# Attention parts ordered one per half unit, units of slice 0 first for two batches, four kv buffers, exponential in place, q loaded in token halves

## The chip, the cores and the metric

The kernel runs on one core of one Trainium2 chip. The metric is the time of one execution on the device in microseconds (us). Before the change it is 1198.53 us, the median of three runs (1197.06 to 1201.19).

## The reference

The program computes three stages in fp32, one after the other.

```python
# attention: B=4 batches, H=8 heads, S=576 tokens, D=64, M=32 memory slots
a  = softmax(phi, over tokens)                      # exp(phi - max), divided by its sum
km = einsum('bhsm,bhsd->bhmd', a, k)                # pooled keys
vm = einsum('bhsm,bhsd->bhmd', a, v)                # pooled values
attn = softmax(q @ km^T / 8)                        # 32 scores for each token and head
x = (attn @ vm) as [2304 tokens, 512]
# first feed-forward: w_in [512, 2048], w_out [2048, 512], given in float64
h = x @ w_in;  x = (h * cos(h)) @ w_out
# second feed-forward: 4 experts, w1 [512, 1024], w2 [1024, 512], weighted by p
out = sum over e of p[:, e] * (relu(x @ w1[e]) @ w2[e])
```

## The kernel before, in words

**Attention.** The eight heads are two groups g of four heads (`HG`). A batch b has four tiles of work in that order: `pool_exp(b, g)` (L173) takes phi, forms the exponential on ScalarE (ACT) and transposes it on TensorE (PE) into `es`; `pool_kv(b, g)` (L193) multiplies `es` by the loaded k and v into `kvp`, scales, transposes and leaves the pooled keys in `kT` and the pooled values in `vT`; `scores(b, g, split_th)` (L225) multiplies `kT` by q, and then runs a softmax as a chain that goes from engine to engine: VectorE (DVE) transposes and takes the maximum, GpSimd (POOL) subtracts, ACT takes the exponential, DVE sums and inverts, POOL multiplies, DVE transposes back, ACT and POOL split the result into a high and a low part (`attnT`). In what follows, a part is `pool_kv(b, g)` with `scores(b, g)`. There are eight parts.

**First feed-forward.** The 2048 hidden columns are cut into eight slices s of 256. A unit is a pair (s, b), and the list `order` (L350) gives the 32 units their sequence; before, slices 0 and 1 of a batch stand one behind the other, batch by batch, and from slice 2 on each slice runs over all four batches. `project(ns)` (L281) folds the pooled values into w_in for one or two units (`vw`). `step1(n, ahead)` (L353) runs a unit in two halves th of 288 tokens: `hidden1` (L303) is 12 matmuls into `hp` and then the cosine on ACT and DVE (its first ACT instruction stands in L319, so L319 counts the halves); `output1` (L327) is 24 matmuls into `op`, added to `acc` by DVE. `output1` runs two halves behind `hidden1` (`pend`). During the attention `op` is one PSUM bank for 128 of the 512 columns, so there are four accumulations a half (128x288); once the attention's PSUM pools are closed, `op` is two banks and there are two accumulations of 128x576. `load_in` and `load_out` (L268, L273) load a slice of weights in two chunks each, and `narrow` (L107) turns float64 into fp32 with one ACT and three DVE instructions a chunk.

**What sets the order.** The program order of the loop at L389 is a priority: the program is planned with a timeline before it runs (L652), and on each engine the earliest instruction in program order that is ready in that timeline is put next. The instructions of several parts and units are thus mixed, and each engine's queue is fixed when the program starts. In the loop, for b = 1 to 3, come both `pool_exp(b, .)`, the unit 2b-2 whole, part (b, 0), part (b, 1), and the unit 2b-1 whole; units 2b-2 and 2b-1 belong to batch b-1. After the loop come the units from 6 on.

**Buffers.** `kv` and `kvt` have three buffers, and a batch uses four (two for each g). `phi` has three and `ex`, the exponential, two. `q` has two, one for a whole batch. All those loads are issued on SyncE's queue (SP), in one sequence.

**Second feed-forward** (L432 to L605) follows, and the change does not touch it.

Of the kernel before, what the change touches and what calls it, by code (L numbers as in the profile page):

```python
# [9 lines left out]
F32 = mybir.dt.float32  # L10
# [14 lines left out]
def tile_kernel(  # L25
# [11 lines left out]
    out: bass.AP,  # L37
):
    nc = tc.nc
    B, HG, S = qt_in.shape[0], qt_in.shape[2], qt_in.shape[3]  # L40
    D = 64
    M = 32
    NT, DM = out.shape
# [100 lines left out]
    cs = cs_ctx.enter_context(tc.tile_pool(name="cs", bufs=2))  # L144
    at_ctx = ExitStack()
    attnT = [mb.tile([128, 2, 2, S], F32R, tag=f"attnT{b}", name="attnT") for b in range(B)]
    vT = mb.tile([128, HG, B, M], F32, tag="vT", name="vT")
    at = at_ctx.enter_context(tc.tile_pool(name="att", bufs=1, side="right"))

    exps = []  # L150
# [7 lines left out]
    def load_kv(b, g):  # L158
        kvs_in[b, g] = []
        for h in range(2):  # L160
            t = at.tile([128, NC, 2, 2 * D], F32, tag="kv", name="kv", bufs=3)
            nc.sync.dma_start(out=t, in_=kv_in[b, g, h])
            t2 = at.tile([TAIL, 2, 2 * D], F32, tag="kvt", name="kvt", bufs=3)
            nc.sync.dma_start(out=t2, in_=kvt_in[b, g, h])
            kvs_in[b, g].append((t, t2))

    def load_q(b):
        qs[b] = at.tile([128, HG, S], F32, tag="q", name="q", bufs=2)
        nc.sync.dma_start(out=qs[b], in_=qt_in[b])

    kTs, ees = {}, {}

    def pool_exp(b, g):  # L173
        ph = phs[b, g]
        nmx = at.tile([128, 1], F32, tag="nmx", name="nmx", bufs=2)
        nc.vector.tensor_reduce(out=nmx, in_=ph, axis=AX.X, op=ALU.max)
        nc.vector.tensor_scalar_mul(nmx, nmx, -1.0)
        ex = at.tile([128, S], F32, tag="ex", name="ex", bufs=2)
        rs = at.tile([128, 1], F32, tag="rs", name="rs", bufs=2)
        nc.scalar.activation(out=ex, in_=ph, func=ACTF.Exp, bias=nmx, accum_out=rs)  # L180
        nc.vector.tensor_scalar_add(rs, rs, 1e-9)
        nc.vector.reciprocal(out=rs, in_=rs)
        es = at.tile([128, NC + 1, 128], F32, tag="es", name="es", bufs=2)
        pe = ps_c.tile([128, NC, 128], F32, tag="c", name="pe")
        for c in range(NC):
            nc.tensor.transpose(pe[:, c, :], ex[:, 128 * c:128 * c + 128], ident)
        nc.scalar.copy(out=es[:, :NC], in_=pe)
        pt = ps_c.tile([128, 128], F32, tag="c", name="pt")
        nc.tensor.transpose(pt[:TAIL], ex[:, 128 * NC:], ident)
        nc.vector.tensor_copy(out=es[:TAIL, NC], in_=pt[:TAIL])  # L190
        ees[b, g] = es, rs

    def pool_kv(b, g):  # L193
        es, rs = ees[b, g]
        kv = kvs_in[b, g]
        p0 = 64 * g
        kvp = ps_c.tile([128, 2 * D], F32, tag="c", name="kvp")
        for c in range(NC + 1):
            n = 128 if c < NC else TAIL
            for i in range(HG):  # L200
                nc.tensor.matmul(  # L201
                    out=kvp[32 * i:32 * i + 32],
                    lhsT=es[:n, c, 32 * i:32 * i + 32],
                    rhs=kv[i // 2][0][:, c, i % 2] if c < NC else kv[i // 2][1][:, i % 2],
                    start=c == 0,
                    stop=c == NC,
                )
        kvs = at.tile([128, 2, 2, D], F32, tag="kvs", name="kvs", bufs=2)
        nc.scalar.activation(
            out=kvs,  # L210
            in_=kvp.rearrange("p (t d) -> p t d", t=2)[:, :, None, :].to_broadcast([128, 2, 2, D]),
            func=ACTF.Copy,
            scale=rs,
        )
        pkt = ps_c.tile([128, 2, 128], F32, tag="c", name="pkt")
        for x in range(2):
            nc.tensor.transpose(pkt[:, x], kvs[:, x].rearrange("p u d -> p (u d)"), ident)
        if g == 0:
            kTs[b] = at.tile([128, HG * M], F32, tag="kT", name="kT", bufs=2)
        nc.vector.tensor_scalar_mul(kTs[b][p0:p0 + 64], pkt[p0:p0 + 64, 0], qk_scale)  # L220
        nc.vector.tensor_copy(
            out=vT[p0:p0 + 64, :, b, :], in_=pkt[p0:p0 + 64, 1].rearrange("p (i m) -> p i m", i=HG)
        )

    def scores(b, g, split_th):  # L225
        aT, p0 = attnT[b], 64 * g
        kT, qT = kTs[b], qs[b]
        st_all = at.tile([128, S // 32, 32], F32, tag="st", name="st", bufs=2)
        smx_all = at.tile([128, S // 32], F32, tag="smx", name="smx", bufs=2)
        ssm_all = at.tile([128, S // 32], F32, tag="ssm", name="ssm", bufs=2)  # L230
# [1 line left out]
        for ths in ((0,), (1,)) if split_th else ((0, 1),):  # L232
            blk = slice(9 * ths[0], 9 * ths[-1] + 9)
            st, smx, ssm = st_all[:, blk], smx_all[:, blk], ssm_all[:, blk]
            nb = st.shape[1]
            for th in ths:
                sc = ps_o.tile([128, 512], F32, tag="o", name="sc")
                for i in range(HG):
                    nc.tensor.matmul(
                        out=sc[32 * i:32 * i + 32, :TH],  # L240
                        lhsT=kT[p0:p0 + 64, 32 * i:32 * i + 32],
                        rhs=qT[p0:p0 + 64, i, th * TH:th * TH + TH],
                        start=True,
                        stop=True,
                    )
                nc.vector.transpose(
                    out=st_all[:, 9 * th:9 * th + 9, :].rearrange("p a b -> p (a b)"), in_=sc[:, :TH]
                )
            nc.vector.tensor_reduce(out=smx, in_=st, axis=AX.X, op=ALU.max)
            nc.gpsimd.tensor_tensor(  # L250
                out=st, in0=st, in1=smx[:, :, None].to_broadcast([128, nb, 32]), op=ALU.subtract
            )
            exps.append(nc.scalar.activation(out=st, in_=st, func=ACTF.Exp))
            nc.vector.tensor_reduce(out=ssm, in_=st, axis=AX.X, op=ALU.add)
            nc.vector.tensor_scalar_add(ssm, ssm, 1e-9)
            nc.vector.reciprocal(out=ssm, in_=ssm)
            nc.gpsimd.tensor_tensor(
                out=st, in0=st, in1=ssm[:, :, None].to_broadcast([128, nb, 32]), op=ALU.mult
            )
            cols = slice(TH * ths[0], TH * ths[-1] + TH)  # L260
            nc.vector.transpose(out=stT_all[:, cols], in_=st.rearrange("p a b -> p (a b)"))
            split(aT[:, 0, g, cols], aT[:, 1, g, cols], stT_all[:, cols], nc.gpsimd)
# [18 lines left out]
    def project(ns):  # L281
        ps = ps_h.tile([128, 2, 512], F32, tag="h", name="vw_ps")
        for j, n in enumerate(ns):
            s, b = order[n]
            for i in range(HG):
                for g in range(2):
                    nc.tensor.matmul(  # L287
                        out=ps[32 * i:32 * i + 32, g, j * FS:j * FS + FS],
                        lhsT=vT[64 * g:64 * g + 64, i, b, :],
                        rhs=wi[s][64 * g:64 * g + 64, i, :],  # L290
                        start=True,
                        stop=True,
# [54 lines left out]
    vws = {}  # L347
    ops_ = [ps_o]
    pend = []
    order = [(s, b) for b in range(B) for s in range(2)]  # L350
    order += [(s, b) for s in range(2, NS1) for b in range(B)]

    def step1(n, ahead):  # L353
        s, b = order[n]
        for th in range(2):
            if n > 8 and b in (1, 2) and s + 1 < NS1:
                (load_in, load_out)[b - 1](s + 1, marks[-1], th)
            pend.append((s, b, th, hidden1(b, th, vws[n]), wo[s]))
            if len(pend) > 2:
                output1(*pend.pop(0))  # L360
            if th == 0 and ahead:
                project(ahead)

    warm = ps_o.tile([128, 512], F32, tag="o", name="warm")
# [1 line left out]
    def warm_up(n):  # L366
        for _ in range(n):
            nc.tensor.matmul(out=warm[:, :128], lhsT=ones, rhs=ones, start=True, stop=True)  # L368

    load_phi(0)  # L370
    load_kv(0, 0)
# [3 lines left out]
    for g in range(2):  # L375
        pool_exp(0, g)
    load_in(0)
    load_out(0)
    load_in(1)
    load_phi(1)  # L380
    for g in range(2):
        pool_kv(0, g)
        scores(0, g, True)
    load_kv(1, 0)
    load_kv(1, 1)
    load_out(1)
    load_q(1)
    project((0, 1))
    for b in range(1, B):  # L389
        if b + 1 < B:  # L390
            load_phi(b + 1)
        pool_exp(b, 0)
        pool_exp(b, 1)
        step1(2 * b - 2, None)
        pool_kv(b, 0)
        if b + 1 < B:
            load_kv(b + 1, 0)
        scores(b, 0, False)
        pool_kv(b, 1)
        if b + 1 < B:  # L400
            load_kv(b + 1, 1)
            load_q(b + 1)
        scores(b, 1, False)
        step1(2 * b - 1, (2 * b, 2 * b + 1))
    nu = 2 * B - 2
    c_ctx.close()
    ps_p2 = p_ctx.enter_context(tc.tile_pool(name="ps_p2", bufs=2, space=PSUM, reuse_waits="tile"))
    ops_[:] = [ps_p2, ps_p2]
# [1 line left out]
    at_ctx.close()  # L410
    wc = ctx.enter_context(tc.tile_pool(name="wc", bufs=2, side="right", reuse_waits="tile"))
    for n in range(nu, len(order)):
        if n == nu:
            load_in(2)
        if n == nu + 1:
            load_out(2)
        step1(n, (n + 1, n + 2) if n % 2 and n + 2 < len(order) else None)
    for p in pend:
# [192 lines left out]
def _layout(q, k, v, phi, moe_w_in, moe_w_out, moe2_domain_probs, moe2_w1, moe2_w2):  # L611
# [6 lines left out]
    kv = np.concatenate([k, v], axis=3).reshape(B, G, 2, I // 2, S, 2 * D).transpose(0, 1, 2, 4, 3, 5)  # L618
    f = moe_w_in.shape[1]
    return {  # L620
        "qt": q.reshape(B, G, I, S, D).transpose(0, 1, 4, 2, 3).reshape(B, G * D, I, S),
        "kv": kv[:, :, :, :n].reshape(B, G, 2, n // 128, 128, I // 2, 2 * D).transpose(0, 1, 2, 4, 3, 5, 6),
        "kvt": kv[:, :, :, n:],
        "phi": phi.reshape(B, G, I, S, M).transpose(0, 1, 2, 4, 3).reshape(B, G, I * M, S),
# [32 lines left out]
```

## Time and profile before

| | us |
|---|---|
| median of three runs | 1198.53 (1197.06 to 1201.19) |
| the profiled execution's own time | 1199.46 |
| its span, first to last instruction | 1197.7 |
| PE busy | 1154.0 (96%) |
| DVE busy | 822.7 (69%) |
| POOL busy | 519.1 (43%) |
| ACT busy | 471.5 (39%) |

The span is the time on the chip between the first and the last instruction; the profiled execution's own time is 1.76 us more. An engine's busy share is an average over stages with different limits, so it has to be looked at stage by stage. All times of the trace count from the span's start.

### The profile page before, as it was taken

To read this page: it belongs to the slowest core of one execution; us is meant where nothing else is said; L and a number is where in the kernel's file an instruction comes from. 1 tells how busy PE (TensorE), PEld (TensorE's weight loads), DVE (VectorE), ACT (ScalarE), POOL (GpSimd) and SP (SyncE) were. 2 spreads that over 40 slices of the span, in tenths; PEclk is the share of its full clock that TensorE was granted. 3 is DMA by queue.
4 is the path that set the end of the run, shared out by engine and by line. 5 is a ranking of instruction groups with operands and counts; after the bars stand their busy time and mean duration, and the time that the engine had idled before them with its cause. 6 is when DMAs were issued, how large, how long until landed. Compare 5 with 4: busy or idle time off the path is not lost.

```text
span 1197.7 us, 19388 instructions
## 1 busy us (share of the span) xinstructions
PE 1154.0 (96%) x7786; PEld 1034.2 (86%) x7786; DVE 822.7 (69%) x1375; ACT 471.5 (39%) x786; POOL 519.1 (43%) x597
## 2 busy tenths in 40 slices
PE   6889789999999989999999999999999999999998
PEld 4477689999999888888989898988898889989897
DVE  5976858788878886666666666697666666665665
ACT  3673646666657543222322222253223222322220
POOL 2543433233336715434544454447345534544420
PEclk7599899999999989999999999999999999999999
DMA  9820102211212201111111111113111111111102
GB/s 332 288 92 21 36 1 72 67 39 38 71 38 70 71 1 53 37 36 54 53 36 36 53 54 36 36 56 129 36 39 53 52 36 53 53 37 36 54 1 79
DMA packets 38267, 72.85 MB, mean 61 GB/s; under 512 B 2561, under 2 KB 20001, under 8 KB 37665
## 3 DMA queue, kind: packets, MB, share of 16 engines
q1 hardware_dynamic: 33632, 58.99, 15.0%
q10 hardware_dynamic: 4480, 12.58, 3.2%
q8 instruction: 61, 1.00, 0.4%
q0 software_dynamic: 64, 0.04, 0.1%
q14 instruction: 30, 0.24, 0.1%
HBM read 66.88 MB, written 4.72 MB: 60 GB/s over the span
## 4 chain that ended last, share of the span: by engine, by line
PE 85%; DVE 4%; DMA 4%; POOL 3%; issue 2%; ACT 2%; POOLq 0%; ACTq 0%; DVEq 0%
PE op L132 46%; PE hp L132 36%; DMA kv<-in_kv_dram 1%; PE vw_ps L287 1%; DMA raw<-in_w_out_dram 1%; DMA raw<-in_w_in_dram 1%; PE kvp L201 1%; POOL wa L491 1%; POOL gt L89 1%; PE warm L368 1%; DMA raw<-in_w_dram 1%; DVE y L321 0%; DVE y L323 0%; DVE acc L343 0%; DVE raw L118 0%
## 5 line engine op out<-in xcount | busy, mean ns | idle before, releaser
L132 PE MATMUL op<-wb,ht 128*128 128x512 f32 x1728 | 439.9, 396 | 0.0
L132 PEld LDWEIGHTS hp<-x,wa 128*128 128x128 f32 x2688 | 380.6, 189 | 24.0 <-DVE x L448 3.5
L132 PE MATMUL hp<-x,wa 128*128 128x320 f32 (+1 forms) x2688 | 393.3, 295 | 3.1 <-DVE x L448 3.1
L132 PEld LDWEIGHTS op<-wb,ht 128*128 128x128 f32 x1728 | 313.2, 188 | 58.6
L580 DVE SCALAR_TENSOR_TENSOR acc<-op,p_all,acc 128x512 f32<-128x512 f32 x270 | 201.7, 748 | 136.9 <-PE op L132 136.7
L132 PE MATMUL op<-gt,wo 128*128 128x288 f32 x1536 | 227.2, 299 | 9.0 <-DVE acc L343 6.9
L132 PEld LDWEIGHTS op<-gt,wo 128*128 128x128 f32 x1536 | 211.1, 189 | 20.4 <-DVE acc L343 8.6
L96 POOL TENSOR_TENSOR wb<-raw,wb 128x256 fp32r<-128x256 f32 x124 | 90.0, 758 | 224.4 <-ACT wb L94 224.4
L551 ACT ACTIVATE ht<-c 128x256 fp32r<-128x256 f32 (+3 forms) x128 | 71.8, 562 | 283.4 <-DVE c L521 283.4
L89 POOL TENSOR_TENSOR gt<-y,gt 128x576 fp32r<-128x576 f32 x64 | 97.6, 1525 | 190.7 <-ACT gt L88 149.5
L552 DVE SCALAR_TENSOR_TENSOR ht<-c,ht 128x256 fp32r<-128x256 f32 (+3 forms) x128 | 94.5, 738 | 63.0 <-ACT ht L551 63.0
L491 POOL TENSOR_TENSOR wa<-raw,wa 128x256 fp32r<-128x256 f32 x96 | 69.2, 749 | 149.8 <-ACT wa L481 149.8
L132 PE MATMUL hp<-attnT,vw 128*128 128x288 f32 x768 | 119.8, 305 | 9.6 <-DVE y L323 9.6
L132 PEld LDWEIGHTS hp<-attnT,vw 128*128 128x128 f32 x768 | 110.5, 196 | 13.0 <-DVE y L323 8.4
L521 DVE TENSOR_TENSOR c<-hp,u 128x256 f32<-128x256 f32 (+1 forms) x192 | 87.3, 457 | 42.3 <-PE hp L132 37.8
L491 POOL TENSOR_TENSOR wa<-tt,wa 128x256 fp32r<-128x256 f32 x128 | 111.4, 900 | 1.2 <-ACT wa L485 1.2
L345 DVE TENSOR_TENSOR acc<-op,acc 128x576 f32<-128x576 f32 (+1 forms) x120 | 84.9, 711 | 29.4 <-PE op L132 28.2
L528 ACT COPY p<-hp 128x256 f32<-128x256 f32 x64 | 25.5, 399 | 112.9 <-PE hp L132 112.9
L321 DVE SCALAR_TENSOR_TENSOR y<-kk,y 128x576 f32<-128x576 f32 x64 | 55.0, 859 | 15.1 <-ACT kk L320 14.7
L319 ACT ACTIVATE y<-hp 128x576 f32<-128x576 f32 x64 | 41.4, 647 | 47.1 <-PE hp L132 40.1
L481 ACT ACTIVATE wa<-raw 128x512 fp32r<-128x512 f32 x32 | 20.2, 632 | 87.5 <-PE hp L132 85.3
L323 DVE TENSOR_TENSOR y<-hp,y 128x576 f32<-128x576 f32 x64 | 48.0, 750 | 9.1 <-ACT y L322 8.4
(89 smaller groups left out, 914.6 us busy)
## 6 DMA issues: line engine op xcount, KB each, us to landing
raw<-in_w_dram SPq DMA_DIRECT2D x60, 512.0 KB, 3.5
kv<-in_kv_dram SPq DMA_DIRECT2D x16, 512.0 KB, 5.3
raw<-in_w_in_dram ACTq DMA_DIRECT2D x10, 512.0 KB, 3.3
raw<-in_w_out_dram ACTq DMA_DIRECT2D x10, 512.0 KB, 3.3
q<-in_qt_dram SPq DMA_DIRECT2D x4, 1152.0 KB, 8.0
out_dram<-acc SPq DMA_DIRECT2D x18, 256.0 KB, 2.0
raw<-in_w_in_dram SPq DMA_DIRECT2D x6, 512.0 KB, 5.4
raw<-in_w_out_dram SPq DMA_DIRECT2D x6, 512.0 KB, 4.9
```

Source lines behind the costliest of these rows:

```text
L89: (eng or nc.vector).tensor_tensor(out=lo, in0=src, in1=f32(hi), op=ALU.subtract)
L96: (nc.vector if early and c % 512 else nc.gpsimd).tensor_tensor(out=t[:, 1, c:c + 256], in0=src[:, c:c + 256], in1=f32(t[:, 0, c:c + 256]) ...
L132: nc.tensor.matmul(out=ps, lhsT=lt(a), rhs=rt(b), start=first and i == 0, stop=last and i == 2, skip_group_check=more,)
L319: marks.append(nc.scalar.activation(out=y, in_=hv, func=ACTF.Copy, scale=INV_2PI, bias=0.25))
L321: nc.vector.scalar_tensor_tensor(out=y, in0=kk, scalar=ROUND, in1=y, op0=ALU.subtract, op1=ALU.subtract)
L323: nc.vector.tensor_tensor(out=y, in0=hv, in1=y, op=ALU.mult)
L345: nc.vector.tensor_tensor(out=dst, in0=op[:, :, :TH], in1=dst, op=ALU.add)
L491: pool.tensor_tensor(out=wa[:, 1, o], in0=src, in1=f32(wa[:, 0, o]), op=ALU.subtract)
L521: nc.vector.tensor_tensor(out=out, in0=ps[:, :n], in1=sb, op=ALU.add)
L551: nc.scalar.activation(out=ht[:, 0, fc, lo:], in_=c[:, fc, lo:], func=ACTF.Relu)
L552: nc.vector.scalar_tensor_tensor(out=ht[:, 1, fc, lo:], in0=c[:, fc, lo:], scalar=0.0, in1=f32(ht[:, 0, fc, lo:]), op0=ALU.max, op1=ALU.su ...
L580: nc.vector.scalar_tensor_tensor(out=dst, in0=op, scalar=pe, in1=dst, op0=ALU.mult, op1=ALU.add)
```

## The change

The program order of the attention and the first units is written out by hand. A part now alternates with half a unit, and a unit needs a batch that is at least one or two behind the part next to it. The sequence of units becomes (0,0), (0,1), (1,0), (1,1), (0,2), (1,2), (0,3), (1,3). Three whole units (six halves) stand within the attention, where six stood before. `kv` and `kvt` get four buffers, the exponential is written over phi, q comes in two tiles of 288 tokens a batch (four buffers of half the size), and `vT` is one tile for each batch. The loads of slice 2 stay at units 6 and 7.

```diff
-    vT = mb.tile([128, HG, B, M], F32, tag="vT", name="vT")
+    vT = [mb.tile([128, HG, M], F32, tag=f"vT{b}", name="vT") for b in range(B)]
...
-            t = at.tile([128, NC, 2, 2 * D], F32, tag="kv", name="kv", bufs=3)
+            t = at.tile([128, NC, 2, 2 * D], F32, tag="kv", name="kv", bufs=4)
...
     def load_q(b):
-        qs[b] = at.tile([128, HG, S], F32, tag="q", name="q", bufs=2)
-        nc.sync.dma_start(out=qs[b], in_=qt_in[b])
+        for th in range(2):
+            qs[b, th] = at.tile([128, HG, TH], F32, tag="q", name="q", bufs=4)
+            nc.sync.dma_start(out=qs[b, th], in_=qt_in[b, th])
...
-        ex = at.tile([128, S], F32, tag="ex", name="ex", bufs=2)
+        ex = ph
...
-    order = [(s, b) for b in range(B) for s in range(2)]
+    order = [(0, 0), (0, 1), (1, 0), (1, 1), (0, 2), (1, 2), (0, 3), (1, 3)]
...
-    def step1(n, ahead):
+    def step1(n, ahead, ths=(0, 1)):
...
+    def part(b, g):
+        pool_kv(b, g)
+        scores(b, g, b == 0)
...
     load_in(0)
+    load_phi(1)
+    part(0, 0)
+    load_kv(1, 0)
     load_out(0)
+    part(0, 1)
+    load_kv(1, 1)
+    load_q(1)
+    project((0,))
+    for g in range(2):
+        pool_exp(1, g)
     load_in(1)
-    load_phi(1)
+    load_phi(2)
+    part(1, 0)
+    load_kv(2, 0)
+    step1(0, None, (0,))
+    load_out(1)
+    part(1, 1)
+    load_kv(2, 1)
+    load_q(2)
     for g in range(2):
-        pool_kv(0, g)
-        scores(0, g, True)
-    load_kv(1, 0)
-    load_kv(1, 1)
-    load_out(1)
-    load_q(1)
-    project((0, 1))
-    for b in range(1, B):
...
-    nu = 2 * B - 2
+        pool_exp(2, g)
+    step1(0, (1,), (1,))
+    load_phi(3)
+    part(2, 0)
+    load_kv(3, 0)
+    step1(1, (2, 3), (0,))
+    part(2, 1)
+    load_kv(3, 1)
+    load_q(3)
+    for g in range(2):
+        pool_exp(3, g)
+    step1(1, None, (1,))
+    part(3, 0)
+    step1(2, None, (0,))
+    part(3, 1)
+    step1(2, None, (1,))
+    nu = 3
```

## Rows read from the trace of the kernel before

**Rows 1.** The page, the span in 40 equal slices, in tenths.

```profile
PE   6889789999999989999999999999999999999998
...
PEclk7599899999999989999999999999999999999999
```

**Rows 2.** Stretches of the first stage; the header names the columns, (x) are instructions.

```profile
core 0: us, PE busy (x) PEld busy (x) DVE busy (x) ACT busy (x) POOL busy (x), PEclk, DMA share, GB/s
13.00:127.00 114.00, 93.34 (x890) 67.35 (x889) 85.86 (x183) 65.12 (x104) 45.77 (x41) 0.84 0.47 162
127.00:165.00 38.00, 27.58 (x193) 25.52 (x174) 25.29 (x42) 19.01 (x28) 14.71 (x11) 0.87 0.09 28
16.00:55.00 39.00, 27.34 (x224) 16.26 (x224) 33.86 (x84) 19.42 (x37) 15.13 (x18) 0.52 0.92 323
55.00:127.00 72.00, 63.80 (x638) 50.26 (x643) 50.99 (x98) 45.06 (x68) 30.64 (x23) 1.00 0.20 65
170.00:390.00 220.00, 218.04 (x1852) 209.13 (x1851) 179.43 (x254) 140.65 (x210) 85.44 (x67) 1.00 0.17 54
```

**Rows 3.** Timeline of ACT: start, us, what; halves 10 and 16, a table load.

```profile
121.53 1.28 ACT L322 ACT_TABLE_LOAD   x1
...
126.96 0.65 ACT L319 ACTIVATE y<-hp 128x576 f32<-128x576 f32 x1 [1.27 <-PE sc L239]
...
174.97 0.65 ACT L319 ACTIVATE y<-hp 128x576 f32<-128x576 f32 x1
```

**Rows 4.** Chain of waits: start, us, what; the start and 178 to 189 us.

```profile
12.91 11.95 DMA kv<-in_kv_dram
...
178.07 1.60 PE hp L132 x12
179.67 3.20 PE op L132 x24
...
187.65 1.02 PE vw_ps L287 x32
```

**Rows 5.** Timeline, the pooled keys of part (0, 1); in brackets the idle time before.

```profile
24.91 1.92 PE L201 MATMUL kvp<-kv,es 128*32 128x128 f32 x28 [4.44 <-DMA kv<-in_kv_dram]
```

**Rows 6.** DVE by line, 13 to 127 us: count, busy, mean ns.

```profile
L118 DVE SCALAR_TENSOR_TENSOR raw<-raw 128x512 uint32<-128x512 uint32 x10 | 10.0, 1004 | 0.2
L321 DVE SCALAR_TENSOR_TENSOR y<-kk,y 128x576 f32<-128x576 f32 x10 | 9.0, 904 | 3.2 <-ACT kk L320 3.2
L323 DVE TENSOR_TENSOR y<-hp,y 128x576 f32<-128x576 f32 x10 | 7.5, 751 | 3.6 <-ACT y L322 3.6
L345 DVE TENSOR_TENSOR acc<-op,acc 128x288 f32<-128x288 f32 x16 | 7.2, 451 | 4.1 <-PE op L132 3.9
L343 DVE COPY acc<-op 128x288 f32<-128x288 f32 x16 | 7.0, 444 | 4.2 <-PE op L132 4.2
L246 DVE STREAM_TRANSPOSE st<-sc 128x288 f32<-128x288 f32 x14 | 6.4, 471 | 2.6 <-PE sc L239 2.5
L117 DVE TENSOR_SCALAR raw<-raw 128x512 uint32<-128x512 uint32 x10 | 5.2, 524 | 3.7 <-DMA raw<-in_w_out_dram 2.9 <-DMA raw<-in_w_in_dram 0.6
...
L89 DVE TENSOR_TENSOR vw<-vw_ps,vw 128x1024 fp32r<-128x1024 f32 x3 | 3.7, 1222 | 1.5 <-ACT vw L88 1.5
```

**Rows 7.** Timeline of PE and ACT, 124 to 157 us, at the last parts.

```profile
124.35 1.85 PE L132 MATMUL hp<-attnT,vw 128*128 128x288 f32 x12 [0.48 <-DVE y L323]
...
127.44 0.74 PE L239 MATMUL sc<-q,kT 64*32 64x288 f32 x8
...
133.23 3.25 PE L132 MATMUL hp<-attnT,vw 128*128 128x288 f32 x12 [3.50 <-DVE y L323]
...
141.75 1.86 PE L132 MATMUL op<-gt,wo 128*128 128x288 f32 x12 [1.89 <-DVE acc L343]
...
156.50 0.65 ACT L319 ACTIVATE y<-hp 128x576 f32<-128x576 f32 x1 [6.81 <-PE hp L132]
```

**Rows 8.** Queue of SP, 0 to 170 us: total wait, times, longest.

```profile
SPq L162 <- PE kvp L201: 42.4, 9, 19.8
```

More of the change, by code (lines that the diff above doesn't have):

```diff
@@ L39, in tile_kernel @@
     nc = tc.nc
-    B, HG, S = qt_in.shape[0], qt_in.shape[2], qt_in.shape[3]
+    B, HG, S = qt_in.shape[0], qt_in.shape[3], 2 * qt_in.shape[4]
     D = 64
@@ L160, in load_kv @@
         for h in range(2):
-            t = at.tile([128, NC, 2, 2 * D], F32, tag="kv", name="kv", bufs=3)
+            t = at.tile([128, NC, 2, 2 * D], F32, tag="kv", name="kv", bufs=4)
             nc.sync.dma_start(out=t, in_=kv_in[b, g, h])
-            t2 = at.tile([TAIL, 2, 2 * D], F32, tag="kvt", name="kvt", bufs=3)
+            t2 = at.tile([TAIL, 2, 2 * D], F32, tag="kvt", name="kvt", bufs=4)
             nc.sync.dma_start(out=t2, in_=kvt_in[b, g, h])
@@ L221, in pool_kv @@
         nc.vector.tensor_copy(
-            out=vT[p0:p0 + 64, :, b, :], in_=pkt[p0:p0 + 64, 1].rearrange("p (i m) -> p i m", i=HG)
+            out=vT[b][p0:p0 + 64], in_=pkt[p0:p0 + 64, 1].rearrange("p (i m) -> p i m", i=HG)
         )
@@ L226, in scores @@
         aT, p0 = attnT[b], 64 * g
-        kT, qT = kTs[b], qs[b]
+        kT = kTs[b]
         st_all = at.tile([128, S // 32, 32], F32, tag="st", name="st", bufs=2)
@@ L241, in scores @@
                         lhsT=kT[p0:p0 + 64, 32 * i:32 * i + 32],
-                        rhs=qT[p0:p0 + 64, i, th * TH:th * TH + TH],
+                        rhs=qs[b, th][p0:p0 + 64, i, :],
                         start=True,
@@ L288, in project @@
                         out=ps[32 * i:32 * i + 32, g, j * FS:j * FS + FS],
-                        lhsT=vT[64 * g:64 * g + 64, i, b, :],
+                        lhsT=vT[b][64 * g:64 * g + 64, i, :],
                         rhs=wi[s][64 * g:64 * g + 64, i, :],
@@ L349, in tile_kernel @@
     pend = []
-    order = [(s, b) for b in range(B) for s in range(2)]
+    order = [(0, 0), (0, 1), (1, 0), (1, 1), (0, 2), (1, 2), (0, 3), (1, 3)]
     order += [(s, b) for s in range(2, NS1) for b in range(B)]
-    def step1(n, ahead):
+    def step1(n, ahead, ths=(0, 1)):
         s, b = order[n]
-        for th in range(2):
+        for th in ths:
             if n > 8 and b in (1, 2) and s + 1 < NS1:
@@ L360, in step1 @@
                 output1(*pend.pop(0))
-            if th == 0 and ahead:
+            if th == ths[0] and ahead:
                 project(ahead)
@@ L377, in tile_kernel @@
     load_in(0)
+    load_phi(1)
+    part(0, 0)
+    load_kv(1, 0)
     load_out(0)
-    load_in(1)
-    load_phi(1)
-    for g in range(2):
-        pool_kv(0, g)
-        scores(0, g, True)
-    load_kv(1, 0)
-    load_kv(1, 1)
-    load_out(1)
-    load_q(1)
-    project((0, 1))
-    for b in range(1, B):
[L390 to L404, printed above, removed]
-    nu = 2 * B - 2
+    part(0, 1)
[4 more added lines that the diff above has]
+        pool_exp(1, g)
+    load_in(1)
+    load_phi(2)
[6 more added lines that the diff above has]
+    load_q(2)
+    for g in range(2):
+        pool_exp(2, g)
[15 more added lines that the diff above has]
+    nu = 3
     c_ctx.close()
@@ L412, in tile_kernel @@
     for n in range(nu, len(order)):
-        if n == nu:
+        if n == 6:
             load_in(2)
-        if n == nu + 1:
+        if n == 7:
             load_out(2)
@@ L620, in _layout @@
     return {
-        "qt": q.reshape(B, G, I, S, D).transpose(0, 1, 4, 2, 3).reshape(B, G * D, I, S),
+        "qt": q.reshape(B, G, I, 2, S // 2, D).transpose(0, 3, 1, 5, 2, 4).reshape(B, 2, G * D, I, S // 2),
         "kv": kv[:, :, :, :n].reshape(B, G, 2, n // 128, 128, I // 2, 2 * D).transpose(0, 1, 2, 4, 3, 5, 6),
```

## The prediction

> **What bounds the kernel now.** I read the slices of the page first. PE is at 9 in nearly every slice but the first five (0 to 150 us), and the granted clock is at its full level everywhere but in slices 1, 2 and 5 [rows 1]. Full level is 2.4 GHz, a row near 0.5 is 1.2 GHz. So the kernel is bound by PE, except in the attention with the first units. The stretches say how far: from 170 to 390 us, units one after the other, PE idles 220 - 218.04 = 2.0 us; from 13 to 127 us it idles 114 - 93.34 = 20.7 us, and from 127 to 165 us 38 - 27.58 = 10.4 us [rows 2]. No other engine is full there: DVE, the busiest, has 85.86 / 114 = 75% and then 25.29 / 38 = 67%. This stage is set by chains between engines, with DVE the nearest to a limit, and by the order in which PE has something to fill the waits with.
>
> The second view is the timeline of ACT, in which each half starts with one L319. The eleventh (half 10) is at 126.96 us, the seventeenth (half 16, the first of slice 2) at 174.97 us [rows 3]. What a half costs PE when nothing is late comes from the chain of waits: 1.60 us for `hidden1`, 3.20 us for `output1`, 1.02 us for `project` of two units [rows 4]. Between the two L319 lie six `hidden1`, six `output1` and two projections: 6 x 1.60 + 6 x 3.20 + 2 x 1.02 = 30.8 us of work in 48.0 us. So 17.2 us are lost after 127 us, when the last score matmuls are already through (127.44 + 0.74 = 128.2 us) [rows 7]. The rows show how: unit 5 waits for accumulations (1.89 us) and for the cosine (3.50 us), and unit 6 needs the last batch, whose `attnT` is not there: its first ACT instruction comes after 6.81 us of idle ACT, at 156.50 us [rows 7]. Before, units 6 and 7 follow directly on the batch that they need.
>
> **What the change removes and moves.** Only the stage up to half 16 can change; from there on program and data are as before. So I estimate how much earlier half 16 comes, and start from t, the time of the last score matmuls, 127 us before.
>
> DVE work up to t. It was busy 85.86 us of 13 to 127 us [rows 2]. After the change there are six `hidden1` up to there where there were ten (L321 and L323), four `output1` where there were eight (32 accumulations in L343 and L345), and projections worth two whole ones where there were three. The chunks of slice 2 that DVE began early (two of ten in L117 and L118) are no longer due. That takes away 4 x (0.904 + 0.751) = 6.6, 16 x 0.45 = 7.2, 1 x 1.22 = 1.2 and 2 x (1.004 + 0.524) = 3.1 us [rows 6], together 18.1; two transposes of 0.47 us (L246 counts 14 of 16) come in. Left are 85.9 - 18.1 + 0.9 = 68.7 us. At the same share of 75.3% that is 91.2 us, so t = 104.2 us.
>
> The fourth `kv` buffer. The fourth tile of batch 0 is issued at 12.91 us, once part (0, 0) has freed a buffer, behind the loads put in front of it, and takes 11.95 us [rows 4]; PE idles 4.44 us for it and starts at 24.91 us [rows 5]. With four buffers it is issued with the other three, and part (0, 1) can run about 10 us earlier. DVE was busy 33.86 of 39 us from 16 to 55 us all the same [rows 2], so most of that only moves work forward. Worth between 0 and 10 us; I take 3, nearer to the low end because DVE was that full, and t becomes 101 us.
>
> Position reached at t. Six `hidden1` and four `output1` are then done instead of eleven and eight. The missing five, four and one projection cost PE 5 x 1.60 + 4 x 3.20 + 1.02 = 21.8 us at the steady rate. So the state of 127 us is reached at 101 + 21.8 = 122.8 us, a gain of 4.2 us: the shorter attention pays back only a little more than the units that are pushed out of it.
>
> The end of the attention. Batch 3 is now first needed by unit 6, and units 3, 4 and 5, which need batches 1 and 2, stand between. That is six halves of 4.8 us, 29 us of PE work; from the last score matmuls to the first ACT instruction of unit 6 it was 156.50 - 128.2 = 28 us before [rows 7], so the tail of the softmax fits beside it, and I count the 17.2 us as gone. What comes late next is the change to two-bank outputs, which still waits for the attention's PSUM (the 1.89 us row is such a wait for accumulations [rows 7]), and the narrowing of slice 2, which moves among units without attention; there DVE has 179.43 of 220 us [rows 2], so it fits. I take 3 us for both together, between 0 and twice the 3.50 us row.
>
> **Edits that I cost at nothing.** Exponential in place: same instruction, but a phi buffer is now held until its transposes; cover is that phi is loaded a whole batch ahead, and if that is gone a `pool_exp` waits for a load. I bound it by 0 and the one load shown with its length, 12 us. Loads of q in halves: four more issues on SP, behind which `kv` and weights queue; SP waited 42.4 us for `kv` buffers in 170 us [rows 8], so issue time is not what is short; the first half can land earlier. Bounds: -1 to +2 us, by the idle rows of about that size [rows 5, 7]. `vT` for each batch takes away a possible false order; no wait of that kind shows in the rows, so 0. Alternating parts and halves makes ACT change its table more often, perhaps four more loads of 1.28 us [rows 3]; ACT is busy 65.12 of 114 us [rows 2], and if that cover failed it would be 4 x 1.28 = 5 us. `load_kv` waits for `pool_kv` of the batch before, and with it all that follows on SP: w_in and w_out of slice 1, phi, q. With four buffers that wait is for the same g of the batch before, a whole `pool_exp` earlier than needed.
>
> **The sum.** 4.2 + 17.2 - 3 = 18.4 us. From the profiled execution's own 1199.46 us (span 1197.7 and 1.76 around it) that gives 1181; the median of the runs lies 0.9 us below that execution, so I forecast 1180 us.
>
> **Rivals.**
>
> The clock (slower). With six halves less among the parts PE has less to do in the attention, pauses between bursts, and the clock falls to its lower level there. For it: after the idle 3.50 us the same twelve matmuls took 3.25 us instead of 1.85 us [rows 7], and from 16 to 55 us, PE 70% busy, the mean granted clock was 0.52 [rows 2]. Against it: from 55 to 127 us, PE 89% busy, it was 1.00 [rows 2]. The changed stage lies between. PE's busy time of 93.34 us falls by 5 x 1.85 + 4 x 3.20 + 1.02 = 23 us to 70 us, in 88 us, which is 80%. About 40 us of that are left after 55 us (70 less 27 from 16 to 55 us, less some 3 before). At 3.25 / 1.85 = 1.76 times that is 30 us more: 1210 us. It decides the sign from 18.4 / 0.76 = 24 us of this work at the lower level. The Trainium skill ("TensorE: Matmul & The Clock Gate", section "Loop structure matters more than you think") has this as a rule: it is the loop nest that decides whether the matmuls keep the full clock, and a wait between bursts loses it. The rows on the twelve matmuls agree with it; by the rule the change would come out at these 1210 us.
>
> The chain (no change). A part is a sequence of a dozen steps on four engines. If these set the pace, fewer units beside them shorten nothing: DVE's share falls instead. At 63% t is 13 + 68.7 / 0.63 = 122 us, and after the 3 us of `kv` 119 us, 18 us later than forecast: 1198 us. The planned order being much the same as before, whatever the program order says, would give the same. For it: DVE idles 28 us from 13 to 127 us although units were there to be done; POOL, at 45.77 of 114 us, waits too [rows 2]. Against it: from 16 to 55 us DVE did reach 33.86 / 39 = 87% with few units beside.
>
> The fuller start (faster). If the early `kv` tiles and units that never wait for the newest batch let DVE keep those 87% up to t, t is 13 + 68.7 / 0.87 = 92 us: 9 us before the forecast, 1171 us. With a clock that comes back before 55 us it would be a few less, so 1169.
>
> **How the numbers follow.** Forecast 0.52 (1180, its own range 1170 to 1190), fuller start 0.20 (1169), chain 0.12 (1198), clock 0.16 (1210). A measurement of this kernel can tell about 0.3% (3.6 us) from no change. Faster by more: 0.52 + 0.20 and a part of the chain's, 0.75. Within: most of the chain's, 0.10. Slower: the clock's with its milder forms cut off, 0.15. The range goes from 1163, where the fuller start comes with the full 10 us of the `kv` tile, to 1200, which leaves the clock out.
>
> **What would show it.** Right: part (0, 1)'s `kvp` matmuls before 18 us; the last score matmuls near 101 us; DVE's share from 13 us to there near 75%; the L319 of half 16 near 156.6 us, and no idle ACT of some 7 us ahead of unit 6; the rest of the trace shifted as a whole. Wrong: a granted clock well under 1.00 between 55 us and the last parts; last score matmuls after 119 us; or new idle time of PE for weights or `kv` on SP's queue that eats the gain.

## The result and the profile after

The changed kernel takes 1185.03 us (median of four runs, 1183.52 to 1186.62) against 1197.8 us before, measured beside it: a ratio of 0.9887, 95% interval 0.9869 to 0.9905. That is 12.8 us less by the medians and some 13.5 us by the ratio. The forecast was 1180 us, a gain of 18.4. The direction and the range hold, and the gain is some 5 us smaller than forecast; what holds of the mechanism stands behind the experiments.

The slices of the page, as in [rows 1] and counted from 0: the dip of PE in slice 4 (120 to 150 us) is gone, and the lower clock stays in slices 0 to 2.

```profile
PE   6798999999999989999999999999999999999998
...
PEclk8689999999999999999999999999999999999999
```

The stretches of the changed kernel, columns as in [rows 2]:

```profile
core 0: us, PE busy (x) PEld busy (x) DVE busy (x) ACT busy (x) POOL busy (x), PEclk, DMA share, GB/s
13.00:100.00 87.00, 70.69 (x742) 45.23 (x735) 70.46 (x160) 57.46 (x92) 42.33 (x38) 0.77 0.63 216
13.00:55.00 42.00, 29.68 (x348) 16.79 (x337) 29.91 (x79) 26.06 (x45) 16.33 (x19) 0.70 0.97 339
55.00:100.00 45.00, 41.02 (x402) 28.44 (x398) 40.56 (x82) 31.40 (x48) 26.00 (x20) 0.84 0.30 100
100.60:162.15 61.55, 57.39 (x451) 54.33 (x451) 42.08 (x64) 34.37 (x50) 21.13 (x16) 0.97 0.06 18
103.20:106.30 3.10, 3.08 (x13) 3.08 (x14) 2.48 (x4) 0.34 (x1) 1.90 (x2) 0.54 0.00 0
```

And its timeline at the places that answer to [rows 3, 5, 7] (L201, L239 and L319 of before are now L202, L240 and L320):

```profile
15.97 1.08 PE L202 MATMUL kvp<-kv,es 128*32 128x128 f32 x32
...
99.43 1.17 PE L240 MATMUL sc<-q,kT 64*32 64x288 f32 x16 [1.25 <-DVE acc L344]
...
102.45 0.72 DVE L324 TENSOR_TENSOR y<-hp,y 128x576 f32<-128x576 f32 x1
...
103.09 0.83 DVE L247 STREAM_TRANSPOSE st<-sc 128x288 f32<-128x288 f32 x2
...
103.22 3.08 PE L132 MATMUL hp<-attnT,vw 128*128 128x288 f32 x12 [2.62 <-DVE y L324]
...
112.61 1.87 PE L132 MATMUL hp<-attnT,vw 128*128 128x288 f32 x12 [1.23 <-DVE y L324]
...
162.15 0.66 ACT L320 ACTIVATE y<-hp 128x576 f32<-128x576 f32 x1 [0.58 <-PE hp L132]
```

Half 16 starts its cosine at 162.15 us instead of 174.97 us: 12.8 us earlier. What follows is as long as before, from there to the end of the span (1197.7 - 174.97 = 1022.7 us, 1184.3 - 162.15 = 1022.2 us). So the whole gain is made ahead of half 16, and the place where the rest of the forecast went can be found by counting. Between the last score matmuls (end 100.6 us) and half 16, PE has these matmuls of the first feed-forward, one line each for `hp`, `op` and `vw_ps` (columns: stretch and its length, PE busy with the count in brackets, PEclk, DMA share, GB/s):

```profile
100.60:162.15 61.55, 19.16 (x120) 0.97 0.06 18
...
100.60:162.15 61.55, 37.86 (x266) 0.97 0.06 18
...
100.60:162.15 61.55, 3.41 (x64) 0.97 0.06 18
```

At the prices of [rows 4] that is 10 x 1.60 + 11.1 x 3.20 + 2 x 1.02 = 53.5 us of work in 61.55 us: 8.0 us are lost there (11.1 is 266 / 24). PE idles 4.2 of them, since all its matmuls together keep it busy for 57.4 us; the other 3.9 us are matmuls that took longer than at these prices. The same count for the kernel before gives 30.1 us of work in 46.8 us, 16.7 us lost (17.2 in the forecast, by program order).

### The profile page after: what moved, and what is told of

Read it like the earlier page. It is cut to its first block, busy times and chain, and to the rows that moved or that the text cites. A ratio compares the mean times of both kernels' runs of the same rounds, so it can differ in the third digit from the quotient of the medians.

```text
span 1184.3 us, 19402 instructions
## 1 busy us (share of the span) xinstructions
PE 1149.7 (97%) x7786; PEld 1029.5 (87%) x7786; DVE 816.6 (69%) x1364; ACT 474.0 (40%) x789; POOL 520.8 (44%) x597
## 4 chain that ended last, share of the span: by engine, by line
PE 83%; DVE 5%; DMA 4%; POOL 3%; ACT 3%; issue 2%; SPq 0%; POOLq 0%; ACTq 0%; DVEq 0%
PE op L132 46%; PE hp L132 35%; DMA raw<-in_w_out_dram 2%; PE vw_ps L288 1%; POOL gt L89 1%; DMA q<-in_qt_dram 1%; POOL wa L505 1%; DVE x L462 1%; DMA kvt<-in_kvt_dram 1%; DVE raw L118 1%; DVE y L324 0%; ACT L323 0%; DVE raw L117 0%; DMA raw<-in_w_in_dram 0%; POOL wo L96 0%
## 5 line engine op out<-in xcount | busy, mean ns | idle before, releaser
L132 PE MATMUL hp<-x,wa 128*128 128x256 f32 (+1 forms) x2688 | 393.6, 295 | 4.1 <-DVE x L462 3.4
L132 PE MATMUL op<-gt,wo 128*128 128x288 f32 x1536 | 224.1, 299 | 2.2 <-POOL gt L89 1.2
L132 PE MATMUL hp<-attnT,vw 128*128 128x288 f32 x768 | 117.1, 300 | 5.1 <-DVE y L324 5.1
L132 PEld LDWEIGHTS hp<-attnT,vw 128*128 128x128 f32 x768 | 107.2, 190 | 10.2 <-DVE y L324 6.6
L346 DVE TENSOR_TENSOR acc<-op,acc 128x576 f32<-128x576 f32 x112 | 83.7, 751 | 24.0 <-PE op L132 22.6
L322 DVE SCALAR_TENSOR_TENSOR y<-kk,y 128x576 f32<-128x576 f32 x64 | 56.9, 890 | 12.9 <-ACT kk L321 12.3
L320 ACT ACTIVATE y<-hp 128x576 f32<-128x576 f32 x64 | 41.4, 647 | 36.1 <-PE hp L132 31.7
L323 ACT ACTIVATE y<-y 128x576 f32<-128x576 f32 x64 | 43.7, 682 | 29.2 <-DVE y L322 29.1
```

The source lines that it names most:

```text
L132: nc.tensor.matmul(out=ps, lhsT=lt(a), rhs=rt(b), start=first and i == 0, stop=last and i == 2, skip_group_check=more,)
L320: marks.append(nc.scalar.activation(out=y, in_=hv, func=ACTF.Copy, scale=INV_2PI, bias=0.25))
L322: nc.vector.scalar_tensor_tensor(out=y, in0=kk, scalar=ROUND, in1=y, op0=ALU.subtract, op1=ALU.subtract)
L323: nc.scalar.activation(out=y, in_=y, func=ACTF.Sin, scale=-TWO_PI)
L346: nc.vector.tensor_tensor(out=dst, in0=op[:, :, :TH], in1=dst, op=ALU.add)
```

## The experiments

Times are medians of their own runs, ratios to the kernel before. "Lost behind the last scores" is always that count: time from the end of the last score matmuls to half 16, less the work in it.

**Which part of the change makes the gain.** First the buffers without the order.

In words: the order of before, with four buffers for `kv` and `kvt`, the exponential written over phi, q in halves and `vT` for each batch.

> The program order of before with all four buffer edits of the change (four kv buffers, exponential in place, q in token halves, one vT for each batch). Theory, the order makes the gain: 1195 to 1199 us, since batch 3 is still needed at once by unit 6 and the 17 us behind the last score matmuls stay. Rival, the early fourth kv tile makes the gain: 1190 us or less, with the pooled keys of part (0, 1) before 18 us instead of 24.91 us and all that follows shifted with them.

1194.01 us, ratio 0.9953 (0.9937 to 0.9970). The theory's bound was missed by 1 us: with the old order the buffers are worth some 5.6 us. But the hole ahead of unit 6 stays, as the timeline of this kernel shows for the first halves of units 6 and 8: ACT idles 6.56 us before unit 6, and 14.7 us are lost behind the last scores.

```profile
153.39 0.65 ACT L320 ACTIVATE y<-hp 128x576 f32<-128x576 f32 x1 [6.56 <-PE hp L132]
...
170.64 0.66 ACT L320 ACTIVATE y<-hp 128x576 f32<-128x576 f32 x1
```

Then the order without the buffers.

In words: the order and the unit sequence of the change, with three buffers for `kv`, two for the exponential, two for a whole q, and one `vT`.

> The program order and unit sequence of the change with the buffers of before (three kv buffers, an exponential of its own, q whole, one vT). Theory, the order makes the gain: 1184 to 1190 us, last score matmuls within 5 us of the 100.6 us of the changed kernel. Rival, the buffers make the gain: 1195 us or more, last score matmuls 8 us later or more.

1186.17 us, ratio 0.9889 (0.9866 to 0.9912): the whole gain, from the order alone. The timeline of this kernel shows something that neither expectation had: the last scores end at 107.9 us, 7 us later than in the changed kernel and so outside the 5 us expected, and yet half 16 comes at the same time.

```profile
107.20 0.69 PE L239 MATMUL sc<-q,kT 64*32 64x288 f32 x8
...
162.33 0.65 ACT L319 ACTIVATE y<-hp 128x576 f32<-128x576 f32 x1 [0.58 <-PE hp L132]
```

Two more `hidden1` are done by then, and only 4.1 us are lost behind. The end of the attention is not by itself what the time hangs on.

**Alternation, or work left over.**

```diff
-    step1(0, None, (0,))
+    step1(0, None)
...
-    nu = 3
+    nu = 6
```

That is a whole unit behind each part, six units among the parts instead of three (`nu`), and the old unit sequence; the loads of slice 1's w_in also stand earlier, ahead of the first projection.

> The changed kernel's buffers and its alternation, but with a whole unit behind each part instead of half a unit, so six units among the parts, in the unit sequence of before, in which unit 6 needs the last batch at once. Theory, the gain is the work left over between the last scores and the first unit of batch 3: it is gone here, 1192 to 1196 us like the buffers alone (1194.0), with 14 us or more lost behind the last score matmuls. Rival, the alternation of parts and units makes the gain: 1184 to 1188 us.

1191.13 us, ratio 0.9929 (0.9910 to 0.9949): between the two. The timeline shows the wait of unit 6 again, 5.10 us, but only 7.6 us are lost behind the last scores, not 14. (The profiled execution, 1188.86 us, is among the fastest of its six, which go from 1188.28 to 1194.85 us.) So alternation may be worth a part, but the interval overlaps with that of the buffers alone, so this is not shown.

```profile
146.07 0.65 ACT L320 ACTIVATE y<-hp 128x576 f32<-128x576 f32 x1 [5.10 <-PE hp L132]
```

```diff
-    order = [(0, 0), (0, 1), (1, 0), (1, 1), (0, 2), (1, 2), (0, 3), (1, 3)]
+    order = [(s, b) for b in range(B) for s in range(2)]
```

> The changed kernel with the unit sequence of before, (0,0), (1,0), (0,1), (1,1) and so on, still three units among the parts. Theory, what counts is that six halves lie between the last part and batch 3: 1184 to 1187 us, no change. Rival, slice 0 first for two batches is needed, because slice 1's weights come late: first half of unit 1 later, 1188 to 1192 us.

1186.36 us, ratio 0.9889 (0.9874 to 0.9905). The sequence of the units makes no difference. Against the run with six units, which has the same sequence and the same buffers, this one is 4.8 us faster, with intervals that do not meet: that much goes with the halves that are left over (and with the earlier w_in, which no run tries alone). It is not the whole gain of some 13 us, and the runs do not divide the rest cleanly: 5.6 us came with the buffers under the old order, and nothing that can be measured under the new one.

In words: four halves among the parts instead of six, the first of them behind part (1, 1), and `nu = 2`.

> The changed kernel with two units (four halves) among the parts instead of three, each half behind the next part. Theory, the gain comes from work left over behind the last scores, and four more halves than needed are already there: nothing more to win, and PE has less to fill the parts with: 1185 to 1190 us, clock lower before the last scores, which come 3 to 6 us earlier. Rival, fewer units among the parts go on paying: 1182 us or less.

1189.02 us, ratio 0.9911 (0.9890 to 0.9932): nothing more to win, as the theory had it, and the clock from 55 to 100 us fell to 0.79. The last scores did not come earlier, though (100.6 us, as with three units).

**Where the missing 5 us went.** Five tries on the places that looked late.

```diff
-                sc = ps_o.tile([128, 512], F32, tag="o", name="sc")
+                sc = ps_c.tile([128, 512], F32, tag="c", name="sc")
```

> The changed kernel with the scores tile in the PSUM pool of the pooling (tag c) instead of the pool of the outputs (tag o). Theory, the last scores hold both output banks until DVE has transposed them, so that PE idles 2.6 us behind them, falls to the lower clock and idles again: 1180 to 1182 us, no idle of PE over 1 us from 100 to 113 us. Rival, PE waits there for the hidden tiles that DVE and ACT have not read yet, whatever bank the scores are in: 1184 to 1187 us; worse, up to 1192 us, if the pooling now waits for its banks.

1188.04 us, ratio 0.9903 (0.9881 to 0.9924). No gain. Behind the last scores the longest idle time of PE is now 1.52 us, and 4.8 us are lost instead of 8.0, but the last scores end at 115.5 us. Before them the pooling does wait for scores in its banks, though for 2.0 us of idle PE in all; why the last scores come 15 us later is not shown.

```diff
-            if th == ths[0] and ahead:
+            if th == (ths[-1] if n == 3 else ths[0]) and ahead:
```

> The changed kernel with the projection of units 4 and 5 traced behind the second half of unit 3 instead of the first. In the changed kernel it is issued at 97.08 us, right before the last scores, and holds one of the two hidden PSUM tiles to about 105 us, while PE idles 2.62 us for the other. Theory, that tile is the cause of the idle time and of the lower clock behind it: 1181 to 1183 us, under 5 us lost behind the last scores instead of 8.0. Rival, ACT and DVE run late there with or without it (two table loads, accumulations ahead in the queue): 1184 to 1187 us.

1187.65 us, ratio 0.9901 (0.9883 to 0.9919). The idle time of 2.62 us behind the last scores is gone, so its cause was the tile, but the time is not won: 10.3 us are lost behind the last scores, where under 5 were expected. The timeline of PE has an idle time of that kind again later: units 4 and 5 are projected behind the scores, and the next projection's split then comes late on DVE, behind the narrowing of slice 2.

```profile
102.02 1.96 PE L288 MATMUL vw_ps<-wi,vT 64*32 64x256 f32 x32 [1.01 <-DVE y L324]
...
134.89 2.50 PE L132 MATMUL hp<-attnT,vw 128*128 128x288 f32 x12 [2.06 <-DVE vw L89]
```

```diff
     load_kv(0, 0)
+    load_q(0)
     load_kv(0, 1)
-    load_q(0)
```

> The changed kernel with the q of batch 0 loaded between the kv tiles of group 0 and group 1. In the changed kernel the chain of waits holds 9.66 us for q (9.52 to 19.18 us), and the first scores start at 17.2 us instead of 14.7 us. If the start sets the pace of the attention: first scores about 15 us, last score matmuls 2 to 3 us earlier, 1182 to 1183 us. If DVE and the loads that follow set it: 1184 to 1186 us, the same within the noise.

1185.32 us, ratio 0.9879 (0.9855 to 0.9902): the same within the noise, with the first scores at 15.05 us and the last ending at 100.4 us.

```diff
-            raw = cw.tile([128, c, 2 * m], U32, tag="raw64", name="raw64")
+            raw = cw.tile([128, c, 2 * m], U32, tag="raw64", name="raw64", bufs=3)
...
-            t = at.tile([128, NC, 2, 2 * D], F32, tag="kv", name="kv", bufs=4)
+            t = at.tile([128, NC, 2, 2 * D], F32, tag="kv", name="kv", bufs=3)
```

> The changed kernel with the fourth kv buffer given back for a third buffer of the weight chunks. In the changed kernel w_out of slice 0 waits for the chunks of w_in (issued at 31.04 us, landed at 38.47 us), and the first output matmuls start at 64.79 us. If late weights leave PE without outputs and so at the lower clock from 50 to 70 us: first outputs 5 us or more earlier, 1180 to 1183 us. If the planned order of the parts, DVE and the full DMA set the pace there: 1184 to 1187 us.

1190.74 us (1186.52 to 1192.33), ratio 0.9918 (0.9893 to 0.9942), above both expected ranges. The first outputs came at 70.84 us, later and not earlier (64.79 us in the changed kernel); PE waits for the fourth `kv` tile again (5.08 us, up to 25.94 us), but why the outputs come later is not shown. That late weights cost time is so neither shown nor excluded. Loading slice 1 later moved as little:

```diff
-    load_in(1)
...
-    load_out(1)
...
     part(2, 0)
+    load_in(1)
...
+    load_out(1)
     part(3, 0)
```

> The changed kernel with the weights of slice 1 loaded later: w_in behind part (2, 0), w_out ahead of part (3, 0). From 10 to 50 us DMA is full (share 0.97) and DVE narrows those weights there. If loads and narrowing of slice 1 set the pace of the first parts: last scores 4 to 8 us earlier, and, since the earlier end of the attention alone gave nothing in the kernel with the buffers of before, 1180 to 1184 us. If the parts' own chains set it: 1184 to 1187 us; if unit (1, 0) now waits for its weights: 1188 us or more.

1186.4 us, ratio 0.9886 (0.9867 to 0.9906), with the DMA share still at 0.97 from 13 to 55 us and the last scores later, at 110.7 us.

**The clock, or DVE.** The clock first.

```diff
                 sc = ps_o.tile([128, 512], F32, tag="o", name="sc")
+                for _ in range(6 if b in (1, 2) else 0):
+                    nc.tensor.matmul(out=sc[:, 384:], lhsT=ones, rhs=ones, start=True, stop=True, skip_group_check=True)
```

> The changed kernel with six added matmuls (128x128, of ones, into unused columns) ahead of each scores tile of batches 1 and 2, most of which the plan puts between 21 and 52 us, where PE idles or runs at the lower clock. They add nothing to the result. If the lower clock (0.50 from 50 to 60 us, 0.53 from 60 to 70 us) sets the pace there: clock up by 0.2 or more, 1181 to 1184 us in spite of some 4 us of added PE work. If DVE, ACT and DMA set it: 1185 to 1190 us, and the clock alone is no cause of what is still lost.

1187.76 us, ratio 0.9907 (0.9882 to 0.9931). The stretches of this kernel show that the clock did come up, from 0.70 to 0.84 and from 0.84 to 0.92, and no time was won with it:

```profile
13.00:55.00 42.00, 32.80 (x340) 23.82 (x340) 30.41 (x81) 24.57 (x43) 12.28 (x15) 0.84 0.97 343
55.00:100.00 45.00, 38.91 (x402) 28.92 (x402) 36.83 (x73) 28.81 (x46) 27.79 (x24) 0.92 0.31 100
```

That is less than the 0.2 asked for, and the added matmuls cost PE time themselves: the 96 of them kept it busy for 15.1 us up to 110 us, and not for the 4 us expected. The last scores end at 108.4 us. So raising the clock in this way gave no more than the matmuls that raise it took; the run does not say that the clock is worth nothing.

Then less work for DVE:

```diff
+            if not after and wn[0] < 8:
+                wn[0] += 1
+                nc.vector.tensor_copy(out=w[:, i:i + c], in_=hif)
+                continue
```

One copy takes the place of L117, L118 and L121 for the eight chunks of slices 0 and 1.

> The changed kernel in which the weights of slices 0 and 1 are narrowed with one DVE instruction a chunk instead of three (only the high word is taken, so this part of the weights has other values); eight chunks by some 1.5 us, 12 us less DVE work before the last scores, nothing else changed. If DVE's amount of work sets the pace of the attention, as the forecast's 75% share assumed: last scores 8 us earlier or more, 1175 to 1180 us. If the chains from engine to engine and the plan set it: last scores within 4 us, 1182 to 1187 us, and DVE's share falls instead.

1179.13 us, ratio 0.9831 (0.9807 to 0.9854), with other weights, so it is no version to keep. The last scores did not move (end 100.1 us), which is what the second expectation said, and still half 16 came at 156.26 us, 5.9 us earlier, and the time is in the range of the first. So neither expectation holds whole.

```profile
13.00:100.00 87.00, 68.20 (x718) 44.70 (x718) 61.91 (x148) 60.18 (x95) 40.63 (x40) 0.80 0.62 217
```

```profile
99.45 0.69 PE L246 MATMUL sc<-q,kT 64*32 64x288 f32 x8
...
156.26 0.65 ACT L326 ACTIVATE y<-hp 128x576 f32<-128x576 f32 x1 [0.58 <-PE hp L138]
```

DVE is busy 8.5 us less up to 100 us; one more `hidden1` is done there, and 4.2 us are lost behind the last scores instead of 8.0. This is the only run of the twelve with a time clearly under that of the changed kernel. Of the versions that compute the reference, none beats it: order alone, q first, the old unit sequence and slice 1 late are the same as it within the noise.

## Why the prediction was right, and which term was off

- **What bounds the kernel.** Right. Only the stage ahead of half 16 changed, and the rest moved as a whole. (The fifteenth slice has a clock of 8 as well [rows 1], which the forecast passes over; it lies behind this stage.)
- **Time of the last scores.** Forecast 101 us, measured 100.6, and in good part by luck. DVE did 70.5 us of work at 81% instead of 68.7 at 75%; among other things the two chunks of slice 2 that the forecast struck out, 3.1 us, were still begun before 100 us (L117 and L118 run ten times there, as before, the last two from 71.99 us on). The buffers brought 7 us and not 3. And the step from DVE's amount of work to the time did not hold when it was tried: with 61.9 us of work instead of 70.5 the last scores ended at 100.1 us, and it was DVE's share that fell, to 71%.
- **Position there.** Forecast six `hidden1` and four `output1`, measured seven and three, with one more projection: 1.60 - 3.20 + 1.02 = -0.6 us of difference. The gain up to the last scores comes out as forecast: 27.6 us earlier, less 6.4 + 16.0 + 1.0 us of work not yet done (four `hidden1`, five `output1`, one projection against the state of before), is 4.2 us.
- **The hole at batch 3.** Right: no wait ahead of unit 6 is left (its L320, at 138.99 us, has no idle time before it), and the runs with six units, where that wait is back, stay 6 to 9 us behind by their medians.
- **The term that was mis-sized: 3 us for the end of the attention.** It measured 8.0 us, with an upper bound of 7 us in the forecast. Together with 16.7 instead of 17.2 that is the missing 5.5 us: 4.2 + 16.7 - 8.0 = 12.9 us. The forecast named the two-bank outputs and the narrowing of slice 2, but the first loss is another: at 100.6 us PE idles 2.62 us because both hidden PSUM tiles wait for DVE (one for L324 at 102.45 us, one with the early projection of units 4 and 5), and both output banks hold scores that DVE transposes only at 103.09 us. After it the twelve matmuls take 3.08 us instead of 1.85, and 1.23 us of idle time come at 112.61 us. For these gaps it was free PSUM that PE lacked, which DVE's instructions free; they and the slower matmuls are not the whole 8.0 us, and where the rest of it lies is not shown.
- **The two terms are not independent.** The forecast added a gain up to the last scores and a loss behind them. In the runs the one goes against the other: where the last scores end at 107.9 to 115.5 us (order alone, old unit sequence, scores in the pooling's banks, slice 1 late, held clock), 3.2 to 5.7 us are lost behind them; where they end at 99.4 to 100.6 us (the change, q first, late projection, two units), it is 6.7 to 10.3 us. Clearly off that line is only the run with less DVE work, with 100.1 and 4.2 us; the third weight buffer, at 103.8 and 4.2 us, lies between.
- **The buffers, 3 us.** They bring the last scores 7 us earlier (100.6 against 107.9 us), but at the end they are worth nothing that can be measured beside the new order. The 3 us stood in a sum that came out right only up to the last scores. Their first effect is as forecast: part (0, 1)'s `kvp` matmuls start at 15.97 us.
- **The rivals.** One of the forecast's own signs of being wrong did come: the granted clock was 0.84 from 55 to 100 us, against 1.00 before, with 0.50 from 50 to 60 us (0.77 before) and 0.53 from 60 to 70 us (1.00 before). But from 13 to 55 us it rose, from 0.55 to 0.70, so that over 13 to 100 us it stayed where it was, at 0.77 (0.78 before), and the time did not go the rival's way. Behind the 2.62 us of idle time the granted clock was 0.54, and the twelve matmuls took the 3.08 us. With that the rule of the Trainium skill named there ("TensorE: Matmul & The Clock Gate", section "Loop structure matters more than you think") agrees; the 1210 us worked out from it did not come. The chain rival holds in part: less DVE work did not bring the last scores earlier.
- **What stays open.** That DVE's work limits what is left is suggested by one run (8.5 us less of it gave 5.9 us). Whether it does so by its amount, by what stands in its queue ahead of the instructions that free PSUM, or because the weights are ready sooner (the first half starts there at 34.35 us instead of 39.08) is not told apart. Half 16 lies between 160.6 and 166.6 us in the changed kernel and in the ten runs that alternate parts and units with DVE's full work, wherever the single gaps fall. That is hardly wider than the runs of one kernel (1183.69 to 1189.12 us with slice 1 late); why it is that constant is not shown.

## What to carry to other kernels

When independent work fills the waits of a chain, keep enough of it for behind the chain's end, until the first consumer of its last result; here three units left over were worth 4.8 us, and a chain that ended 7 us earlier nothing that could be measured. Price such a change by the work still to be done at a fixed later point and not by when the chain ends, because here a plan that ended the chain earlier had less done by then and lost more behind it. And look at what frees the filler's buffers: at 100.6 us PE had units left to do and idled 2.62 us until DVE freed a PSUM tile.

## What the runs showed that was not expected

- Less DVE work left the last scores where they were (100.1 us) and still brought half 16 forward by 5.9 us.
- Removing a single idle gap (2.62 us of PE) brought no time: another of 2.06 us appeared 32 us later, behind the same engine.
- Raising the mean granted clock from 0.70 to 0.84 over 42 us, and from 0.84 to 0.92 over the next 45 us, made the kernel no faster, with added matmuls that kept PE busy for 15.1 us.
- The same buffers are worth 5.6 us with the old order and nothing measurable with the new one.
